# A fused attention and mixer kernel: the last 64 rows' sums in 128x32 strips behind the low-rank sums, and another order of the first slot

## The chip, the core and the metric

The kernel runs on one core of a Trainium2 chip. A core has five engines that run side by side, each through its own list of instructions: TensorE (PE) multiplies matrices into the accumulators (PSUM), VectorE (DVE), ScalarE (ACT) and GpSimd (POOL) work on elements, SyncE (SP) issues transfers. They wait for each other by semaphores. The metric is the device time of one execution in microseconds (us), the median of several executions. Three executions of the kernel before gave 979.51, 979.74 and 979.88 us: the median is 979.74 us.

## What is computed

```python
def _attn_ref(u, v, z):                     # u, v: 8 x 3136 x 256, z: 8 x 3136 x 64
    scores = (1.0 / S) * np.matmul(z, z.transpose(0, 2, 1))
    attn = np.maximum(scores, 0.0) ** 2
    return (u * np.matmul(attn, v)).astype(np.float32)

def _moe_ref(x, U, V, w_ch1, w_ch2):        # U: 3136 x 32, V: 32 x 3136
    h = x.transpose(0, 2, 1) @ U @ V
    u = x + h.transpose(0, 2, 1)
    ch = np.maximum(u @ w_ch1, 0.0) @ w_ch2 # 256 -> 1024 -> 256
    return (u + ch).astype(np.float32)
```

The output of the first is x of the second, for 8 batches b of 3136 rows. Matrices are multiplied in bf16 and summed in fp32.

## The kernel before

**Groups and slots.** The 3136 rows of a batch are 24 tiles of 128 rows and a tail of 64. Four tiles make a group, so a batch has six whole groups (g = 0 to 5) and the **small group** (g = NQ = 6) of the 64 tail rows. One (b, g) is an item, and the loop at L1395 runs one slot t for each of the 56 items. A slot holds the attention sums of its own item ("av", L668), the scores of a coming one (L428), the low-rank part of the item 7 slots back (`u2_unit`, L861) and the two channel products `ch1` and `ch2` of the item 8 slots back (L965, L1053).

**Order of the work.** The program is written out in the order in which it is recorded here; nothing reorders it. `emit` (L1159) walks through the slot's list of light units (one unit is a pair of matmuls of the av or the ch2 stream) and puts the units of the other queues in at the places that are given with them, if as many accumulators are free as the entry asks for. The kernel keeps a clock of its own (`clock`, `free_at`, `book`) by which it judges that, and by which `hold` puts off casts, squares and transfers. A matmul of 256 columns counts one unit of that clock.

**Accumulators.** There are four PSUM tiles of two banks (`take_ps`, L148). The av stream of a slot holds one throughout.

**Ways.** Most matmuls use 64 of the 128 rows of the array, two at a time: one on each half, each into another bank (`pair`, L179). To use both halves for both banks the stream goes through its data twice, in two ways (L640). At a change of ways a half must wait until the other half has done with the bank: an empty instruction on POOL (`post`, L170) waits for the last matmul, and the next matmul waits for it. What PE does between the two is one pair of scores or a transposition.

**Scores.** A pair of scores (two matmuls of 512 columns) must be scaled, cut off at zero and squared into bf16. `rectify` (L366) does so in one of three ways: "both" (ACT scales and cuts off, DVE squares), "dve" (DVE does both steps in two instructions, L397), "act" (ACT does both, L380, L381). In slot 0 it takes the ways that the list `ways` (L105) names, and when that is empty the one that the kernel's clock gives as the earliest. Batch 0 has nothing prepared, so in slot 0 the av stream uses blocks of scores just made, and z is turned on PE in four pieces (`z_turn`, L325); its last piece is the tail, whose casts `cast_tail` (L1314) makes on DVE. The six pieces of v of batch 0 are cast on POOL (L1307).

**The small group.** Its 64 rows are handled apart. `av_small` (L727) sums its attention in 52 matmuls on 64x64 quarters of the array, and `ch2_small` (L1139) its second channel product in 16; `four_sums` (L756) brings the four partial sums together (a copy on ACT, two additions on DVE). In the first slot of batches 2 to 7 both stand at place 72 of the av stream (L1474), `ch2_small` for the small group of two batches earlier. `t1_all` (L818) makes the low-rank sums U^T x of the batch before in 28 matmuls on four 128x32 strips of the array, at place 8 of the same slot (L1506); ACT copies half of the result, DVE adds the halves and doubles them (L847 to L849), and `u2_unit` at place 22 uses it. The batch's last piece of v is cast to bf16 in that slot too, by ACT (`cast`, L204).

Of the kernel before, what the change touches and what calls it, by code (L numbers as in the profile page):

```python
# [18 lines left out]
def kernel(  # L19
# [24 lines left out]
    GT = 4  # L44
# [60 lines left out]
    ways = ["both", "dve"]  # L105
# [260 lines left out]
    def rectify(dst, src, b, part=1, whole=False):  # L366
# [24 lines left out]
        return book("act", ready, 8.7 if part == 1 else 5.3), None  # L391
# [335 lines left out]
    def av_small(b, g):  # L727
        k, ps = take_ps()
        rows = groups[g][1]
        xs[b, g] = pool.tile([P, 1, D], BF16, name="x_small")  # L730
        nc.vector.memset(xs[b, g][rows:, 0, :], 0.0)
        for jt in range(NQ + 1):
            while (b, jt) not in v_cast:
                run_held(min(h[0] for h in held))
        for jt in range(NT + 1):
            c = jt % 2
            part = slice(0, D) if jt < NF else slice(c * D // 2, (c + 1) * D // 2)
            at = min(jt, NF)
            for h in range(2):
                nc.tensor.matmul(  # L740
                    out=ps[c * hp : c * hp + rows, h, part],
                    lhsT=smalls[b][h * hp : (h + 1) * hp, place_of(at), :],
                    rhs=v_bfs[b][h * hp : (h + 1) * hp, at, part],
                    start=(jt < 2),
                    stop=(jt >= NF),
                    tile_position=(h * hp, c * hp),
                )
        pe(NT / 2 + 2)
        u1 = u_sbs[b, g]
        four_sums(k, ps, u1[:rows, 1:3, :])  # L750
        nc.vector.tensor_tensor(
            out=xs[b, g][:rows, 0, :], in0=u1[:rows, 1, :], in1=u1[:rows, 0, :], op=ALU.mult
        )
        book("dve", clock[0] + 3, 3)

    def four_sums(k, ps, t):  # L756

        rows = t.shape[0]
        nc.scalar.copy(out=t, in_=ps[hp : hp + rows, :, :D])
        ready = book("act", clock[0] + 3, 5)  # L760
        nc.vector.tensor_tensor(out=t, in0=ps[:rows, :, :D], in1=t, op=ALU.add)  # L761
        ps_free[k] = book("dve", ready + 1, 6)
        nc.vector.tensor_tensor(out=t[:, 0, :], in0=t[:, 0, :], in1=t[:, 1, :], op=ALU.add)
        book("dve", ready, 4)
# [53 lines left out]
    def t1_all(b):  # L818
# [26 lines left out]
        up = pool.tile([P, D], FP32, name="t1_up", bufs=1)  # L845
# [15 lines left out]
    def u2_unit(b, g, turn=True):  # L861
# [145 lines left out]
    def small_relu(b, g):  # L1007

        return flat_of(relus[b, g][0])[:, : NH * groups[g][1]]

    def ch1_small(b, g, way, box):
# [4 lines left out]
        if way == 0:  # L1016
            relus[b, g] = [take_block()]
# [106 lines left out]
    def ch2_out(b, g, acc):  # L1124

        for e in relus.pop((b, g)):
            give_block(e)
# [10 lines left out]

    def ch2_small(b, g):  # L1139
        k, ps = take_ps()  # L1140
        rows = groups[g][1]
        for kt in range(NH):
            c = kt % 2
            for h in range(2):
                nc.tensor.matmul(  # L1145
                    out=ps[c * hp : c * hp + rows, h, :D],
                    lhsT=small_relu(b, g)[h * hp : (h + 1) * hp, kt * rows : (kt + 1) * rows],
# [435 lines left out]
```

## Time and profile before

| | |
|---|---|
| Median of three executions | 979.74 us |
| The profiled execution | 979.08 us |
| Its span, first to last instruction | 977.3 us |
| PE busy | 969.4 us (99%) |
| DVE busy | 633.7 us (65%) |
| ACT busy | 480.0 us (49%) |
| POOL busy | 15.7 us (2%) |
| First 20 us: PE, DVE, ACT, POOL busy | 17.22, 13.44, 15.63, 10.60 us |
| 20 to 40 us: the same | 19.15, 16.97, 17.31, 5.14 us |
| 400 to 600 us: PE busy | 200.00 us |
| 900 to 977 us: PE busy | 72.99 us |
| Granted TensorE clock in every one of these stretches | 1.00 |

The span is what the profiler saw between the first and the last instruction; the time of the execution lies 1.8 us above it. A median can be compared with another median, and a row of the profile with the span.

In a timeline each line gives the start of a row of equal instructions in us from the span's start, the time from the start of the first to the end of the last, the engine, the line of the kernel, the operation, what it writes and reads, the shape, and in brackets how long the engine had been idle before and what released it. A shape of 64\*128 is one on half the rows of the array, 64\*64 one on a quarter, 128\*32 one on a strip. The ends of matmuls overlap with the next ones; the distance between the starts of two rows is what counts.

### The profile page before, as it was taken

The page shows a single profiled execution, that of the slowest core. Times are in us where ns is not written, and L with a number is a line of the kernel's source. Part 1 is how long each engine was busy: PE and PEld are TensorE (multiplying, and loading weights), DVE is VectorE, ACT ScalarE, POOL GpSimd, SP SyncE. Part 2 cuts the span into 40 slices and gives each one's busy share as a digit, 9 for nine tenths or more (in the row PEclk, how much of TensorE's full clock was granted, in tenths as well). Part 3 has the DMA queues.
Part 4 walks back from the last instruction along what each step waited for, and adds up shares of the span by engine and source line. Part 5 has one row for each costly group of instructions (what it writes and reads, how often), then busy time and mean ns, then how long its engine had stood idle before and what let it go on. Part 6 is the DMA issues. An engine that isn't in the chain of part 4 may idle for free.

```text
span 977.3 us, 35450 instructions
## 1 busy us (share of the span) xinstructions
PE 969.4 (99%) x16211; PEld 774.7 (79%) x16211; DVE 633.7 (65%) x815; ACT 480.0 (49%) x562; POOL 15.7 (2%) x25
## 2 busy tenths in 40 slices
PE   8999999999999999999999999999999999999998
PEld 6798777887778777787778877788777888778765
DVE  6887865668556775557756577556765667653363
ACT  8877732457334563345543365433653346531353
POOL 4200000000000000000000000000000000000000
PEclk9999999999999999999999999999999999999999
DMA  9999899989988799997999679996999968974142
GB/s 271 193 202 223 207 208 209 201 192 182 198 211 161 182 197 189 210 147 186 182 222 195 139 185 198 213 185 131 198 213 202 192 133 183 179 137 101 50 116 98
DMA packets 372549, 176.37 MB, mean 180 GB/s; under 512 B 347312, under 2 KB 350896, under 8 KB 372400
## 3 DMA queue, kind: packets, MB, share of 16 engines
q1 hardware_dynamic: 372256, 173.98, 87.2%
q8 instruction: 126, 2.06, 0.9%
q14 instruction: 23, 0.19, 0.1%
q10 hardware_dynamic: 144, 0.13, 0.0%
HBM read 62.56 MB, written 25.69 MB: 90 GB/s over the span
## 4 chain that ended last, share of the span: by engine, by line
PE 98%; DVE 1%; ACT 0%; issue 0%; DVEq 0%
PE ps L184 95%; PE ps L740 1%; PE ps L825 1%; PE ps L1145 0%; ACT blk L390 0%; DVE blk L364 0%; PE ps L1349 0%; PE ps L331 0%; DVE blk L553 0%; DVE blk L397 0%; DVE x_bf L775 0%; ACT last_sb L390 0%; DVE blk L1113 0%; PE ps L542 0%; DVE blk L761 0%
## 5 line engine op out<-in xcount | busy, mean ns | idle before, releaser
L184 PEld LDWEIGHTS <-blk 64*128 64x128 bf16 x12288 | 610.9, 94 | 152.6 <-POOLq L174 8.9
L184 PE MATMUL ps<-v_bf,blk 64*128 64x256 bf16 x9216 | 610.2, 269 | 1.0 <-DVE blk L364 0.8
L390 ACT ACTIVATE blk<-ps 128x1024 bf16<-128x1024 f32 (+1 forms) x335 | 313.8, 969 | 344.0 <-PE ps L184 339.0
L364 DVE TENSOR_TENSOR blk<-blk 128x1024 bf16<-128x1024 bf16 x350 | 222.3, 658 | 46.2 <-ACT blk L390 45.6
L184 PE MATMUL ps<-u2T,w_bf 64*128 64x512 bf16 (+1 forms) x1792 | 226.2, 349 | 0.0
L1002 DVE TENSOR_SCALAR blk<-ps 128x1024 bf16<-128x1024 f32 x111 | 135.9, 1224 | 103.7 <-PE ps L184 102.8
L184 PE MATMUL ps<-w_bf,blk 64*128 64x256 bf16 x3072 | 189.8, 269 | 0.0
L1005 ACT ACTIVATE blk<-ps 128x1024 bf16<-128x1024 f32 x81 | 82.2, 1022 | 123.9 <-PE ps L184 120.1
L184 PE MATMUL ps<-zzT 64*128 64x512 bf16 (+2 forms) x898 | 128.1, 326 | 0.6 <-ACT zzT L340 0.6
L184 PEld LDWEIGHTS <-w_bf 64*128 64x128 bf16 x1792 | 82.2, 94 | 27.9 <-POOLq L174 5.2
L775 DVE TENSOR_TENSOR x_bf<-ps,u_sb 128x1024 bf16<-128x1024 f32 x48 | 58.7, 1222 | 68.4 <-PE ps L184 68.4
L910 DVE TENSOR_TENSOR out_sb<-ps,x_bf 128x1024 f32<-128x1024 f32 x42 | 51.4, 1223 | 57.4 <-PE ps L184 57.4
L1131 DVE TENSOR_TENSOR out_sb<-ps,out_sb 128x1024 f32<-128x1024 f32 x42 | 51.4, 1224 | 19.2 <-PE ps L184 19.2
L184 PEld LDWEIGHTS <-zzT 64*128 64x128 bf16 x898 | 41.6, 94 | 6.3 <-ACT zzT L340 0.8
L206 DVE CAST v_bf<-stage 128x1024 bf16<-128x1024 f32 (+1 forms) x35 | 21.5, 615 | 0.0
L386 DVE TENSOR_SCALAR blk<-ps 128x1024 bf16<-128x1024 f32 x14 | 17.1, 1223 | 6.5 <-PE ps L184 5.8
L184 PE MATMUL ps<-t_sb,V_bf 64*128 64x256 bf16 (+1 forms) x208 | 20.3, 265 | 0.0
L204 ACT CAST x_bf<-out_sb 128x1024 bf16<-128x1024 f32 x19 | 19.7, 1037 | 0.0
L184 PE MATMUL ps<-v_bf,last_sb 64*128 64x256 bf16 x192 | 18.5, 269 | 0.0
L1131 DVE TENSOR_TENSOR blk<-ps,blk 128x1024 f32<-128x1024 f32 x5 | 6.1, 1225 | 11.9 <-PE ps L184 11.8
L204 ACT CAST v_bf<-stage 128x1024 bf16<-128x1024 f32 x13 | 13.5, 1040 | 0.0
L626 ACT ACTIVATE attn_small<-ps 128x512 bf16<-128x512 f32 (+1 forms) x32 | 13.1, 499 | 0.0
(86 smaller groups left out, 239.1 us busy)
## 6 DMA issues: line engine op xcount, KB each, us to landing
u_sb<-in_u_dram SPq DMA_DIRECT2D x48, 512.0 KB, 5.1
stage<-in_v_dram SPq DMA_DIRECT2D x42, 512.0 KB, 6.4
out_dram<-out_sb SPq DMA_DIRECT2D x42, 512.0 KB, 3.1
stage<-in_z_dram SPq DMA_DIRECT2D x7, 512.0 KB, 6.3
blk<-in_v_dram SPq DMA_DIRECT2D x5, 512.0 KB, 6.1
out_dram<-blk SPq DMA_DIRECT2D x5, 512.0 KB, 2.8
blk<-blk SPq DMA_TRANSPOSE x156, 5.1
blk<-in_moe_w_ch_dram SPq DMA_DIRECT2D x4, 512.0 KB, 5.5
```

The costliest lines, as they stand in the source:

```text
L184: ins = nc.tensor.matmul(**args)
L204: nc.scalar.copy(out=out, in_=in_)
L206: nc.vector.tensor_copy(out=out, in_=in_)
L364: nc.vector.tensor_tensor(out=a, in0=a, in1=a, op=ALU.mult)
L386: nc.vector.tensor_scalar(out=dst, in0=src, scalar1=scale, scalar2=0.0, op0=ALU.mult, op1=ALU.max)
L390: nc.scalar.activation(out=dst, in_=src, func=AF.Relu, scale=scale)
L626: nc.scalar.activation(out=dst[:, jj], in_=src[:, jj], func=AF.Relu, scale=scale)
L775: nc.vector.tensor_tensor(out=xs[b, g][:rows, :n, :], in0=four(box["ps"])[:rows, :n, :], in1=u_sbs[b, g][:rows, :n, :], op=ALU.mult,)
L910: nc.vector.tensor_tensor(out=o, in0=four(ps), in1=x, op=ALU.add)
L1002: nc.vector.tensor_single_scalar(out=r, in_=ps[:, :, :gw], scalar=0.0, op=ALU.max)
L1005: nc.scalar.activation(out=r, in_=ps[:, :, :gw], func=AF.Relu)
L1131: nc.vector.tensor_tensor(out=o, in0=acc, in1=o, op=ALU.add)
```

## The change

1. `av_small`, `four_sums` and `ch2_small` are replaced by `small_sums`. It makes the sums of the small group on four 128x32 strips (`in_strips`), 32 of the 64 rows to a strip and every second tile to the other pair of strips, as many matmuls of the same columns as before: 16 for the second channel product into bank 0 (argument `second`, a batch), 52 for the attention into bank 1 (argument `first`). One copy, one addition and the final instructions follow.
2. In the first slot of batches 2 to 7 `both_sums` calls `t1_all` and right behind it `small_sums`, at place 8. The channel product is now that of three batches earlier, so the small group's `relu_small` and `out_small` get buffers of their own, which live a batch longer. `u2_unit` moves from place 22 to 12, and the load of `u_small` from 130 units into the slot before to 10. Batches 0 and 1 keep their attention sums where they were, in strips; the last three channel products stand behind `t1_all` of the last batch and in the last part.
3. In the first slot (t = 0) two pairs of scores stand at four of the five changes of ways that had one, and single pairs at five places in the stream where there were nine. `ways` names ten choices instead of two. The kernel's clock counts 9.3 for ACT's step in slots 0 and 1 where it counted 8.7. `cast_tail` casts on POOL.

```diff
     slot = [0]
-    ways = ["both", "dve"]
+    ways = ["both", "dve", "both", "both", "both", "dve", "both", "both", "both", "dve"]
...
         else:
-            t = pool.tile([P, 3, D], FP32, name="u_small", bufs=1)
+            t = pool.tile([P, 1, D], FP32, name="u_small", bufs=1)
...
             dve += 6.5 * waiting[0]
-            ends = {"dve": dve + DVE, "act": act + 19, "both": max(act + 8.7, dve) + 7.5}
+            ends = {"dve": dve + DVE, "act": act + 19, "both": max(act + 9.3, dve) + 7.5}
...
         nc.scalar.activation(out=dst, in_=src, func=AF.Relu, scale=scale)
-        return book("act", ready, 8.7 if part == 1 else 5.3), None
+        return book("act", ready, 5.3 if part != 1 else 9.3 if slot[0] < 2 else 8.7), None
...
-    def av_small(b, g):
+    def in_strips(ps, bank, lhs, rhs, n, odd):
+
+        m = P // NREP
+        for i in range(n):
+            whole = i < n - 1 or not odd
+            for c in range(NREP) if not whole else (i % 2 * 2, i % 2 * 2 + 1):
+                w = c % 2
+                part = slice(0, D) if whole else slice(c // 2 * D // 2, (c // 2 + 1) * D // 2)
+                nc.tensor.matmul(
+                    out=ps[c * m : (c + 1) * m, bank, part],
+                    lhsT=lhs(i, slice(w * m, (w + 1) * m)),
+                    rhs=rhs(i)[:, part],
+                    start=(i < 2),
+                    stop=(i >= n - 2 if not odd else not whole),
+                    tile_position=(0, c * m),
+                )
+        pe(n / 2 + 1)
+
+    def small_sums(second, first, into=None):
+
         k, ps = take_ps()
...
-    def four_sums(k, ps, t):
...
+        rows = groups[NQ][1]
+        if second is not None:
+            in_strips(
+                ps,
+                0,
+                lambda i, w: small_relu(second, NQ)[:, i * rows : (i + 1) * rows][:, w],
+                lambda i: w2_bf[:, i, :],
+                NH,
+                False,
+            )
+        if first is not None:
+            b = first
+            xs[b, NQ] = pool.tile([P, 1, D], BF16, name="x_small")
+            nc.vector.memset(xs[b, NQ][rows:, 0, :], 0.0)
+            for jt in range(NQ + 1):
+                while (b, jt) not in v_cast:
+                    run_held(min(h[0] for h in held))
+            in_strips(
+                ps,
+                1,
+                lambda i, w: smalls[b][:, place_of(i), w],
+                lambda i: v_bfs[b][:, i, :],
+                NT,
+                True,
+            )
+        at, end = 0 if second is not None else 1, 2 if first is not None else 1
+        n = end - at
+        t = (into or sums_tile())[:rows]
+        nc.scalar.copy(out=t[:, at:end], in_=ps[hp : hp + rows, at:end, :D])
+        ready = book("act", clock[0] + 3, 1 + 2 * n)
+        nc.vector.tensor_tensor(out=t[:, at:end], in0=ps[:rows, at:end, :D], in1=t[:, at:end], op=ALU.add)
+        ps_free[k] = book("dve", ready + 1, 1 + 2.5 * n)
+        if first is not None:
+            nc.vector.tensor_tensor(
+                out=xs[first, NQ][:rows, 0, :], in0=t[:, 1, :], in1=u_sbs[first, NQ][:rows, 0, :], op=ALU.mult
+            )
+            book("dve", clock[0] + 3, 3)
+        if second is not None:
+            ch2_out(second, NQ, t[:, 0:1, :])
+            book("dve", clock[0] + 3, 3)
...
-    def t1_all(b):
+    def sums_tile():
+        return pool.tile([P, GT, D], FP32, name="out_sb", bufs=3)
+
+    def both_sums(b, second, first):
+        t = sums_tile()
+        t1_all(b, t)
+        small_sums(second, first, t)
+
+    def t1_all(b, into=None):
...
-        up = pool.tile([P, D], FP32, name="t1_up", bufs=1)
+        up = (into or sums_tile())[:, 2, :]
...
             o = raw.rearrange("p (q d) -> p q d", d=D)
+        elif n < GT:
+            o = pool.tile([P, 1, D], FP32, name="out_small", bufs=2)
...
-        return flat_of(relus[b, g][0])[:, : NH * groups[g][1]]
+        return relus[b, g]
...
         if way == 0:
-            relus[b, g] = [take_block()]
+            relus[b, g] = pool.tile([P, NH * gw], BF16, name="relu_small", bufs=1)
...
-        for e in relus.pop((b, g)):
-            give_block(e)
+        e = relus.pop((b, g))
+        if g < NQ:
+            for x in e:
+                give_block(x)
...
-    def ch2_small(b, g):
...
         for c in range(2):
-            on_dve(out=z_bfs[0][:, NF, c, :], in_=raw[:, 2 * GT * dqk : n * dqk])
-        v_tail(0, n, raw, on_dve)
-        book("dve", clock[0], 5)
+            on_pool(out=z_bfs[0][:, NF, c, :], in_=raw[:, 2 * GT * dqk : n * dqk])
+        v_tail(0, n, raw, on_pool)
...
         if t > NG and g_now == NQ and b_next < B:
-            hold(clock[0] + 60 + 70, lambda b=b_next: load_u(b, NQ))
+            hold(clock[0] + 10, lambda b=b_next: load_u(b, NQ))
...
             if t == NG:
-                qc.append((64, 2, False, lambda: av_small(1, NQ)))
-            if fin:
-                qc.append((72, 2, False, lambda: (ch2_small(*fin), av_small(att[0], NQ))))
+                qc.append((64, 2, False, lambda: small_sums(None, 1)))
             k = min(2, len(mine) // 3)
             n = len(mine) - 3 * k
             at = [1 + 80 * i / n for i in range(n)]
             if t == 0:
-                at, k = [16, 30, 46, 50, 64, 68, 78, 84, 92], 0
+                at, k = [16, 50, 64, 78, 84], 0
                 qs += [(4, 0, True, lambda: scores(1)), (12, 0, True, lambda: z_turn(0, 2 * GT, on_act))]
-                qs += [(x, 0, True, lambda: scores(1)) for x in (24, 40, 56, 72, 88)]
+                qs += [(x, 0, True, lambda x=x: scores(1 if x == 56 else 2)) for x in (24, 40, 56, 72, 88)]
...
-            small = (lambda: None) if early(*att) else (lambda: av_small(*att))
+            small = (lambda: None) if early(*att) else (lambda: small_sums(None, att[0]))
...
                 else:
-                    order = up + [small, c0, c1, d0, d1, c2, c3, lambda: t1_all(att[0]), d2, d3]
+                    order = up + [small, c0, c1, d0, d1, c2, c3, lambda: both_sums(att[0], B - 3, None), d2, d3]
             qc += [(0, 0, False, f) for f in order]
         if av and u2i:
             if u2i[1] == 0:
-                qm.append((8, 1, False, lambda: t1_all(u2i[0])))
-            qm.append((22 if u2i[1] == 0 else 40, 1, False, lambda: u2_unit(*u2i)))
+                sums = t > NG
+                b = att[0]
+                qm.append(
+                    (
+                        8,
+                        2 if sums else 1,
+                        False,
+                        lambda: both_sums(b - 1, b - 3 if b > 2 else None, b) if sums else t1_all(b - 1),
+                    )
+                )
+            qm.append((40 if u2i[1] else 12 if sums else 22, 1, False, lambda: u2_unit(*u2i)))
...
             if k == 1 or k == NQ:
-                qm.append((9, 1, False, lambda b=B - 2 if k == 1 else B - 1: ch2_small(b, NQ)))
+                qm.append((9 if k == 1 else 5, 1, False, lambda b=B - 2 if k == 1 else B - 1: small_sums(b, None)))
```

More of the change, by code (lines that the diff above doesn't have):

```diff
@@ L723, in av_stream @@
         return Ways(2 * NF, 1, step, box)
-    def av_small(b, g):
-        k, ps = take_ps()
[L729 to L754, printed above, removed]
@@ L756, in four_sums @@
-    def four_sums(k, ps, t):
[L758 to L764, printed above, removed]
+    def in_strips(ps, bank, lhs, rhs, n, odd):
[14 more added lines that the diff above has]
+        pe(n / 2 + 1)
@@ L1136, in ch2_out @@
             give_block(o_blocks.pop((b, g)))
-    def ch2_small(b, g):
[L1140 to L1147, printed above, removed]
-                    rhs=w2_bf[h * hp : (h + 1) * hp, kt, :],
-                    start=(kt < 2),
-                    stop=(kt >= NH - 2),
-                    tile_position=(h * hp, c * hp),
-                )
-        pe(NH / 2 + 2)
-        sums = u2s[b, g][:rows, 1:3, :]
-        four_sums(k, ps, sums)
-        ch2_out(b, g, sums[:, 0:1, :])
-        book("dve", clock[0] + 3, 3)
     def emit(light, queues, av=None, slack=14, hurry=14):
```

## The prediction

> **What bounds the kernel now.** I read the page's busy times first, then the chain that ended last, then PE's timeline where the change works.
>
> ```profile
> span 977.3 us, 35450 instructions
> PE 969.4 (99%) x16211; PEld 774.7 (79%) x16211; DVE 633.7 (65%) x815; ACT 480.0 (49%) x562; POOL 15.7 (2%) x25
> ...
> PE 98%; DVE 1%; ACT 0%; issue 0%; DVEq 0%
> ```
>
> PE is the bound and hardly pauses: 7.9 us of the span are idle, of them 3.6 in the first 40 us and 4.0 in the last 77 (mostly the last output on its way). After 40 us PE's busy time equals the time, so a gain there can only come from matmuls that take less time, not from shorter waits. Both programs have 16211 matmuls of the same columns. What can differ is how densely they stand. The timeline of a batch's first slot (b = 2):
>
> ```profile
> 212.36 0.93 PE L184 MATMUL ps<-v_bf,blk 64*128 64x256 bf16 x14
> 213.22 0.84 PE L825 MATMUL ps<-x_bf,U_bf 128*32 128x256 bf16 x24
> 213.89 0.20 PE L835 MATMUL ps<-x_small,U_bf 128*32 128x64 bf16 x4
> 214.02 1.05 PE L184 MATMUL ps<-v_bf,blk 64*128 64x256 bf16 x16
> ...
> 221.91 1.36 PE L184 MATMUL ps<-v_bf,blk 64*128 64x256 bf16 x22
> 223.20 0.63 PE L1145 MATMUL ps<-w_bf,blk 64*64 64x256 bf16 x16
> 223.66 1.54 PE L740 MATMUL ps<-v_bf,attn_small 64*64 64x256 bf16 x52
> 225.13 1.05 PE L184 MATMUL ps<-v_bf,blk 64*128 64x256 bf16 x16
> ```
>
> Compare starts. In the long streams a pair of 256 columns takes 0.1094 us (22 of them: 11 pairs, 1.20). From 221.91 that gives 223.11, but the 64x64 matmuls begin at 223.20: 0.09 lost on entering another division of the array. They are 68 matmuls in fours, 17 x 0.1094 less half a step for the four of 128 columns = 1.81; they took 1.93 up to 225.13. With 0.01 in the first pair behind, a stretch of 64x64 costs 0.23 us beyond its columns. The strips cost the same: 0.09 before 213.22, 0.80 for 0.68 of columns (six fours and 64 columns), 0.01 behind: 0.23. Within a stretch strips and quarters run alike, four matmuls in 0.1094 to 0.112.
>
> In the first slot PE does wait. The chain of waits there:
>
> ```profile
> 16.90 1.55 PE ps L184 x22
> 18.46 0.01 issue
> 18.47 0.23 PE ps L331
> ...
> 20.48 1.02 ACT last_sb L390
> 21.50 2.76 ACT blk L390 x3
> ...
> 24.89 1.22 DVE x_bf L775
> 26.11 0.61 DVE blk L364
> ...
> 26.77 4.63 PE ps L184 x70
> ```
>
> Between 20 and 26 us the chain runs over ACT's scaling and DVE, not over PE: scores are made barely in time. From the starts of PE's rows, the waits for DVE's squares are 0.20 at 16.90, 0.21 at 19.72, 1.01 at 26.77, 0.17 at 31.40 and 0.16 at 32.01 us: 1.75 in all. Five changes of ways with one pair of scores between cost 0.066 us each.
>
> **The change, part by part.**
>
> *Fewer divisions.* Counted in the built programs, stretches of 64x64 or 128x32 fall from 18 to 12: in the first slots of batches 2 to 7 two become one. 6 x 0.23 = **-1.38 us**. The new strips have the form of L825 (128 rows, 32 columns, 256 moving), so I take that row's pace; the weights change as often.
>
> *A cast that is needed sooner.* The attention sums move from place 72 to behind `t1_all`, and need all of v. The last piece is cast by ACT, and the built program puts that cast right behind ACT's copy of the low-rank sums:
>
> ```profile
> 214.15 0.37 ACT L847 COPY t_up<-ps 64x256 f32<-64x256 f32 x1 [0.55 <-PE ps L835]
> ...
> 214.42 1.04 ACT L204 CAST v_bf<-stage 128x1024 bf16<-128x1024 f32 x1
> ```
>
> So v is whole at 215.46, 1.57 after L835's start (213.89). Strips begin 0.03 after that start. In batches 3 to 7 the 16 matmuls of `ch2` go first (0.44), then 40 of attention (1.09) before the 41st needs the piece: 1.56, against 1.57 and some 0.05 for the semaphore: 0.05 lost. In batch 2 there is no `ch2` part: 1.12 against 1.62, 0.50 lost. Sum **+0.75**. Behind PE nothing else of ACT waits then. The bounds are 0, if the clock of the kernel lets the cast go a little earlier, and +1.8, if one of ACT's scalings (1.02, L390) slips in front of it once.
>
> *The results of the sums.* One copy (0.58, L759's form), one addition (0.68) and two short ones (0.42 each) on DVE follow, and in front of `u2_unit`'s addition (1.22). PE's next scores want the accumulator back 1.53 us after the strips end; copy and addition take 0.12 + 0.58 + 0.03 + 0.68 = 1.41. No wait, by 0.1 us; DVE has some 35% of idle time to take the rest. If the cover goes, it is 0.15 a batch. Buffers, the earlier `u_small` load and the stores are SP's; the load lands 5 us after its issue in the profile and has a slot more time, so I put them at nothing, and so the end of the program, where the order of the last pieces on PE, DVE and SP stays.
>
> *The first slot,* by the built program's order and the durations of rows: ACT's scaling 1.02 (the next starts 0.93 later), DVE's two steps 1.22 and 0.69, ACT's square 1.05 (no row; L554's 128x512 square took 0.63 where the same-sized scaling took 0.59, so a little over 1.02; the bounds are 0.9 and 1.2). I number PE's matmuls.
> - Until 145 the two pairs at the change save 0.07. Matmul 147 is the first of a second pair, and needs z's next piece, which ACT had copied at 15.12: it starts at 15.16 where it was free at 14.82. At 165 PE is 0.21 behind; the old wait of 0.20 at 16.90 falls away (DVE's square ends at 16.93), so 183 starts at 17.43, before 17.35.
> - Matmul 197 turns z's tail. Its casts now stand on POOL behind two casts of v:
>
> ```profile
> 17.69 1.23 POOL L1310 CAST v_bf<-blk 128x512 bf16<-128x512 f32 x2 [1.50 <-PE ps L184]
> 17.70 0.71 DVE L1317 CAST z_bf<-blk 128x64 bf16<-128x64 f32 x2
> ```
>
>  POOL's casts of v wait for the same change of ways, so they run 17.77 to 19.00, and z's two follow, at 0.1 each (an eighth of 0.61, and a little): 19.2. PE starts 197 at 19.27, not 18.47: **0.8 behind**.
> - The scores behind it come later too. ACT gets its next pair at 21.18 (20.48 before) and has in order three scalings with their squares, now on ACT, and one more scaling: 7 steps, to 28.26; DVE's square of that pair ends at 28.97, and matmul 318 needs it: 29.03, before 27.43. The waits at 242 (0.4) and 294 (0.4) lie inside that.
> - The old waits at 31.40 and 32.01 shrink to 0.2: matmul 394 at 34.04, before 32.56. One more doubled change saves 0.07. From there nothing waits: **+1.4**.
>
> Bounds: all 1.75 of waits and 4 x 0.066 gone, -2.0; or POOL and DVE slow each other, below, +3.0.
>
> Sum: -1.38 + 0.75 + 1.4 = +0.77 on the profiled execution's 979.08 (977.3 of span and 1.78 around it), 979.85. The median lies 0.66 above that execution, so 980.5.
>
> **The rivals.** I call a difference under 0.2% (1.96 us) no change; a measurement of this kernel tells about that.
> 1. *Faster: the first slot becomes dense.* If the tail's cast is ready at about 18.5 (POOL gets to it before v) and the sharing keeps ACT ahead, the waits of 1.75 and the 0.26 go: 979.74 - 1.38 + 0.75 - 2.0 = 977.1. For it: ACT worked without a pause from 21.40 to 26.33, and three scalings leave it there. Against it: three squares come instead, and the order on POOL is fixed.
> 2. *Slower: POOL and DVE get in each other's way.* In the profile a 128x64 cast on DVE took 0.19 and the next one 0.61 beside POOL's cast, and a square at 28.36 took 1.25 instead of 0.69. If one waits out the other, a square ahead of POOL's second cast of v puts z's tail at 19.9 (+0.7), the squares before 394 are late by 0.5 beside POOL's casts at 29.6 to 32, and those behind by 0.4 beside its casts near 35: 1.4 + 1.6 = 3.0, and 979.74 + 3.0 - 0.63 = 982.1. It decides from +2.6 in the first slot on. Against it: there POOL's two took 0.68 and 0.61. The Trainium skill (SBUF — State Buffer, section "SBUF: two separate sides") says that the port pair which VectorE and GpSimd share is "an **exclusive lock**, not a bandwidth split", held for the whole instruction. By that rule this rival is the rule and not the accident; the 0.61 and the 1.25 agree with it, POOL's undisturbed 0.61 at 18.31 doesn't decide.
> 3. *It does not save the division.* A merged stretch might drain between banks or between `t1_all` and the sums: without the -1.38 the sum is 981.9. Against it: L1145 and L740 follow each other in the profile in another accumulator with no loss.
>
> **How the numbers follow.** Forecast (within 0.2%): 0.43. Rival 1 and other gains: 0.25. Rival 2 0.27, rival 3 0.05, together slower 0.32. The time is 980.5; its own range is 978.6 (first slot at -0.5) to 981.7 (at +2.6, where rival 2 begins). The range over the cases goes from 976.9, just under rival 1, to 982.6, which is rival 2 with the cover of 0.15 lost in three of the six merged stretches.
>
> **What would show it.** Right: six stretches of 80 or 96 strips with one loss of 0.1 at each end; a wait of 0.5 for the cast in batch 2 and hardly any in the others; in the first slot PE waiting for POOL near 19.2 and for a DVE square near 29; no PE wait after 35 us. Wrong: z's tail turned before 18.8; a PE start of 318 before 28; strips slower than 0.115 per four; or waits of PE inside the steady slots, which the profile before has none of.

## The result, and the profile after

The changed kernel took **983.06 us** (median of seven executions, 982.63 to 984.60), the kernel before 979.88 (979.51 to 981.09) beside it on the same chip. The ratio is **1.0033, 95% interval 1.0024 to 1.0043**: slower by about 3.2 us. The prediction had 980.5 and a range of 976.9 to 982.6. The profiled execution of the changed kernel took 983.06.

Its page: span, busy times, and the chain of waits by engine.

```profile
span 981.3 us, 35422 instructions
PE 969.2 (99%) x16211; PEld 798.4 (81%) x16211; DVE 622.6 (63%) x792; ACT 476.4 (49%) x556; POOL 16.1 (2%) x28
...
PE 94%; DVE 1%; ACT 1%; DMA 1%; SPq 0%; issue 0%; DVEq 0%; ACTq 0%
```

PE is busy for 969.2 us where it was 969.4, DVE and ACT are busy for less, POOL for 0.4 more, and the span is 4.0 us longer. So the added time is not added work: PE stands idle for longer, and the chain now goes over DMA too, which it did not before. The view of what PE waited for in the whole span gives the places, first in the kernel before, then in the changed one (zzT holds the turned z, t_sb the low-rank sums, u2T the turned rows that `ch1` multiplies; SPq in other listings is SP issuing a transfer):

```profile
PE ps L184 <- DVE blk L364: 0.8, 1, 0.8
...
PE ps L184 <- ACT zzT L340: 0.6, 1, 0.6
PE ps L331 <- POOL z_bf L242: 0.2, 1, 0.2
```

```profile
PE ps L184 <- DMA u2T<-x_small: 1.7, 1, 1.7
PE ps L331 <- POOL z_bf L1332: 1.4, 1, 1.4
PE ps L184 <- DVE blk L364: 1.3, 2, 1.0
...
PE ps L184 <- ACT zzT L340: 0.4, 1, 0.4
PE ps L735 <- ACT v_bf L204: 0.3, 1, 0.3
PE ps L184 <- ACT blk L380: 0.3, 1, 0.3
PE ps L184 <- DVE t_sb L879: 0.2, 1, 0.2
PE ps L184 <- DVE blk L1035: 0.2, 1, 0.2
```

The columns are: us in total, how often, and the longest. Four of these lie in the first slot (POOL z_bf, DVE blk L364, ACT blk L380, and zzT at 10.4 us, which was 0.6 before). Of the others only v_bf was foreseen: the rest are a transposition that is late near 930 us, t_sb at 99.6 and L1035 at 127.9. What a wait costs is more than the idle time shown, because the profile models the ends of matmuls and idle time counts from them: from start to start, the idle 1.36 at L331 cost 1.52, 0.33 at v_bf cost 0.51, 0.17 at t_sb cost 0.33, 1.73 at u2T cost 1.90, that is 0.165 to 0.176 more each time.

Both programs have the same number of matmuls with the same columns, so the starts of equal places can be subtracted. Distances between starts on PE, in us (the first three by PE's matmul numbers, the others from the first matmul of a batch's low-rank sums to that of the next):

| Stretch | before | after | difference |
|---|---|---|---|
| matmul 145 to 199 (z's tail is turned) | 3.96 | 5.61 | +1.65 |
| 199 to 321 (the scores behind it) | 8.91 | 9.67 | +0.76 |
| 97 to 1400 in all (slots 0 to 6) | 78.78 | 81.04 | +2.26 |
| 1400 to batch 1's low-rank sums | 122.90 | 123.88 | +0.98 |
| batch 1's to batch 2's | 119.50 | 119.65 | +0.15 |
| each next to the one of batch 6 | 119.50 | 119.35 to 119.40 | -0.10 to -0.15 |
| batch 6's to batch 7's | 111.13 | 110.65 | -0.48 |
| batch 7's to the last matmul | 50.89 | 53.21 | +2.32 |

Two rows move work over their edges: `ch2` of a small group (16 matmuls, 0.44) leaves the row of 119.65 and arrives in the last one, and the low-rank sums stand six matmuls later in the order (0.31), which is in the row of 123.88 and comes off at 110.65. Without these: +0.67 in batch 1, +0.59 in the next row, +1.88 at the end.

### The profile page after: what moved, and what is told of

It is laid out like the page before. It is cut to its first block, busy times and chain, and to the rows that moved or that the text cites. A ratio compares the mean times of both kernels' runs of the same rounds, so it can differ in the third digit from the quotient of the medians.

```text
span 981.3 us, 35422 instructions
## 1 busy us (share of the span) xinstructions
PE 969.2 (99%) x16211; PEld 798.4 (81%) x16211; DVE 622.6 (63%) x792; ACT 476.4 (49%) x556; POOL 16.1 (2%) x28
## 4 chain that ended last, share of the span: by engine, by line
PE 94%; DVE 1%; ACT 1%; DMA 1%; SPq 0%; issue 0%; DVEq 0%; ACTq 0%
PE ps L184 92%; PE ps L735 1%; PE ps L856 1%; DVE blk L364 0%; DMA stage<-in_v_dram 0%; DVE blk L1035 0%; DMA u2T<-x_small 0%; ACT blk L390 0%; SPq L220 0%; ACT blk L1038 0%; SPq L412 0%; DVE w_bf L206 0%; ACT v_bf L204 0%; ACT w_bf L204 0%; ACT out_sb L878 0%
## 5 line engine op out<-in xcount | busy, mean ns | idle before, releaser
L184 PEld LDWEIGHTS <-blk 64*128 64x128 bf16 x12288 | 632.6, 94 | 133.4 <-POOLq L174 8.2
L390 ACT ACTIVATE blk<-ps 128x1024 bf16<-128x1024 f32 (+1 forms) x330 | 310.1, 967 | 349.3 <-PE ps L184 331.7
L364 DVE TENSOR_TENSOR blk<-blk 128x1024 bf16<-128x1024 bf16 x348 | 218.4, 653 | 49.2 <-ACT blk L390 48.6
L1035 DVE TENSOR_SCALAR blk<-ps 128x1024 bf16<-128x1024 f32 x111 | 135.9, 1224 | 112.8 <-PE ps L184 112.8
L184 PEld LDWEIGHTS <-w_bf 64*128 64x128 bf16 x1792 | 85.4, 94 | 27.6 <-POOLq L174 5.1
L184 PEld LDWEIGHTS <-zzT 64*128 64x128 bf16 x898 | 44.0, 94 | 6.4 <-ACT zzT L340 1.2
L735 PE MATMUL ps<-v_bf,attn_small 128*32 128x256 bf16 (+1 forms) x416 | 12.9, 269 | 0.3 <-ACT v_bf L204 0.3
```

The costliest lines, as they stand in the source:

```text
L184: ins = nc.tensor.matmul(**args)
L364: nc.vector.tensor_tensor(out=a, in0=a, in1=a, op=ALU.mult)
L390: nc.scalar.activation(out=dst, in_=src, func=AF.Relu, scale=scale)
L735: nc.tensor.matmul(out=ps[c * m : (c + 1) * m, bank, part], lhsT=lhs(i, slice(w * m, (w + 1) * m)), rhs=rhs(i)[:, part], start=(i < 2), st ...
L1035: nc.vector.tensor_single_scalar(out=r, in_=ps[:, :, :gw], scalar=0.0, op=ALU.max)
```

## The experiments

Each ratio is to the kernel before on the same chip, with its 95% interval. Executions on these chips scatter more than in the first runs (the kernel before from 979.3 to 982.5), among other things because matmul 97 starts anywhere from 11.3 to 13.0 us into the span (one profiled execution of each kernel). Distances from matmul 97 on are free of that, and carry the readings below.

### The first slot, and one store at the end

The first kernel takes all edits of the first slot back (item 3 of the change). The second takes nothing back but the place of one store on SP's queue:

```diff
-        nc.sync.dma_start(out=dst, in_=o)
-        queued(n * rows)
+        def store():
+            if (b, g) == (B - 3, NQ) and (B - 2, NQ) not in u2Ts:
+                hold(clock[0] + 1, store)
+                return
+            nc.sync.dma_start(out=dst, in_=o)
+            queued(n * rows)
+
+        store()
```

The third does both, the fourth puts the edits of the first slot alone into the kernel before.

> The changed kernel with the first slot as it was (two given ways, single pairs at the changes, z's tail cast by VectorE, 8.7 in the booking). Theory: the first slot alone lost 2.12 us and nothing else depends on it, so the time is 983.06 - 2.1 = 980.95, and PE still waits 0.33 at the zzT matmuls behind the low-rank sums of batch 0 (99.61 in the changed kernel), 0.32 at the ch1 matmuls near 127.87, and 1.7 for the transposition of x_small near 930. Rival: the two waits of batch 1 come from a clock of the kernel that the first slot shifted; then they go too, 980.3. Second rival: the loss of the first slot is made up again later, and the time stays at 982.5 or above.

> The changed kernel with one DMA moved on SP's queue: the store of batch 5's small group is issued behind the transposition of batch 6's x_small in place of ahead of it; PE's program is the same matmul for matmul. Theory: the transposition waited on SP behind that store, which waits for VectorE's addition ending at 927.0; issued at about 924.3 it lands at 927.6, under the first use, and the 1.90 us that PE lost at 930.05 go: 981.15, the PE wait for u2T<-x_small gone. Rival: the transposition itself is slow there because the DMA engines are busy with stores; then it still lands after 928.3 and PE still waits 0.5 or more: 981.7 to 983.0.

> Both edits: the first slot as it was and the store behind the transposition; what is left of the change is the sums in 128x32 strips and their place. Theory: the two losses lie in different stretches and add up: 983.06 - 2.12 - 1.90 = 979.0, 0.8 under the kernel before, as the five merged stretches of batches 3 to 7 save 0.12 to 0.16 each and the two waits of batch 1 and batch 2's wait for the cast stay. Rival: the strips cost as much as they save, 979.6 to 980.1. Second rival (the waits of batch 1 leave with the first slot): 978.4.

> The kernel before with the first slot's edits alone (the given ways, two pairs at the changes, z's tail cast by GpSimd, 9.3 in the booking); the sums stay in 64x64 quarters in their old places. Theory: the first slot loses 2.12, 982.0, with z's tail turned at 19.9 and PE waiting 1.2 for a square near 29.6. Rival: later waits follow from it too (0.64 in batch 1): 982.6. Second rival: the first slot only loses in company with the other edits: 979.9 to 980.5.

| Kernel | median, us | ratio | matmul 97 to 1400 | batch 7's low-rank sums to the end |
|---|---|---|---|---|
| first slot as before | 981.45 | 1.0012 (1.0003 to 1.0021) | 78.91 | 53.21 |
| store behind the turn | 982.16 | 1.0019 (1.0011 to 1.0028) | 81.09 | 51.59 |
| both | 979.45 | 0.9993 (0.9984 to 1.0003) | 79.05 | 51.53 |
| first slot alone | 982.95 | 1.0027 (1.0016 to 1.0039) | 81.09 | 51.40 |

The two losses are independent and add up, as expected: from matmul 97 to 1400 the first slot costs 2.0 to 2.3 whatever the sums do, and at the end the store costs 1.6 to 1.7. In ratios the theories had 1.0011, 1.0013, 0.9991 and 1.0022. The first and the third came out so; the medians of the second and the fourth lie at or next to their rivals' values (1.0019 to 1.0032, and 1.0028), though the rivals' reasons fit only in part: in the second a small wait is left at the transposition, and in the fourth PE loses 0.18, 0.29 and 0.50 near 129, 348 and 930 us. The timeline at the end of the kernel before, where that transposition leaves as soon as x_small is cast:

```profile
921.60 0.39 ACT L204 CAST x_small<-out_sb 64x256 bf16<-64x256 f32 x1
922.02 1.18 SPq L811 DMA_TRANSPOSE u2T<-x_small  x1
...
925.49 0.40 PE L184 MATMUL ps<-u2T,w_bf 64*128 64x64 bf16 x16
```

In the changed kernel:

```profile
923.84 0.39 ACT L204 CAST x_small<-out_small 64x256 bf16<-64x256 f32 x1
...
926.58 0.42 DVE L1166 TENSOR_TENSOR out_small<-out_sb,out_small 64x256 f32<-64x256 f32 x1
927.02 0.53 SPq L1168 DMA_DIRECT2D out_dram<-out_small  x1
927.66 1.18 SPq L834 DMA_TRANSPOSE u2T<-x_small  x1
...
930.05 0.41 PE L184 MATMUL ps<-u2T,w_bf 64*128 64x64 bf16 x16 [1.73 <-DMA u2T<-x_small]
```

and the same with the store behind the transposition (matmul 97 starts 1.6 us later in it, so compare distances):

```profile
925.47 0.39 ACT L204 CAST x_small<-out_small 64x256 bf16<-64x256 f32 x1
925.89 1.17 SPq L834 DMA_TRANSPOSE u2T<-x_small  x1
...
928.66 0.52 SPq L1172 DMA_DIRECT2D out_dram<-out_small  x1
930.07 0.41 PE L184 MATMUL ps<-u2T,w_bf 64*128 64x64 bf16 x16
```

x_small was ready to be transposed at 924.23. SP takes its queue in order, and in front stood the store of batch 5's small group, which `both_sums` had brought there and which waits for DVE's addition up to 927.00. So the transposition left 3.4 us after its data were ready, and in the second listing at once. PE's program is the same in both. 0.28 of loss is left there, since 4.1 pass from its issue to its landing, where 3.4 passed in the kernel before, which had no wait there. That rest is not the store's: in the ten kernels with strips and the moved store the landing took 3.65 to 4.30 and PE lost 0 to 0.44, and in the fourth kernel, whose sums stand in their old places, it took 3.92 and PE lost 0.50. In the kernel before, it landed 0.06 ahead of PE's start, so the place had no margin to begin with.

The wait for t_sb in batch 1 did not leave with the first slot (0.33 at L879 stands in all three kernels with strips and not in the fourth): it belongs to the sums. The other, at L1035, can't be placed so: its idle time is 0.04, 0.34 and none in the three, and PE loses 0.18 there in the fourth.

### The parts of the first slot

The kernel with both taken back is the base here; to it come, one each: all edits of the slot but the tail's casts; those casts on GpSimd alone; the list `ways` alone; the two pairs at a change alone.

```diff
-            on_dve(out=z_bfs[0][:, NF, c, :], in_=raw[:, 2 * GT * dqk : n * dqk])
-        v_tail(0, n, raw, on_dve)
-        book("dve", clock[0], 5)
+            on_pool(out=z_bfs[0][:, NF, c, :], in_=raw[:, 2 * GT * dqk : n * dqk])
+        v_tail(0, n, raw, on_pool)
```

> Strips and moved store kept, and of the first slot all edits but one: z's tail is cast by VectorE as before. In the run with the first slot as before the time stood 0.7 us under the kernel before; the whole first slot cost 2.12. Theory: GpSimd's late casts (z's tail ready at 19.86, PE losing 1.52 at its turn) are most of the first slot's loss, since the stalls behind it only hand it on: without them 0.6 to 1.0 of the 2.12 is left, and the time is 0.1 under to 0.3 over the kernel before; PE loses under 0.3 at the turn of z's tail. Rival: ACT's chain of three scalings and three squares sets the end of the slot whatever the tail does; then 1.7 to 2.1 is left, 1.0 to 1.4 over the kernel before, with a wait of PE for a square of some 2 us near 29.

> Strips and moved store kept, the first slot as before but for z's tail, which GpSimd casts behind its two casts of v. Theory: POOL's casts of v take 0.85 each beside a square on VectorE, the tail is turned at 19.7 to 19.9, PE loses 1.2 to 1.5 there, and ACT's later scalings, which the kernel before had no pause in, hand on nearly all of it: 0.4 to 0.8 over the kernel before (against 0.7 under it with the whole old slot). Rival: the stall at the tail is taken back at the wait of 1.01 near 26.77, whose length is set by ACT's chain from an earlier point: then 0.2 to 0.7 under the kernel before.

> Strips and moved store kept, the first slot as before but for the list of given ways (ten in place of two; single pairs at the changes, tail on VectorE). Theory: sharing by the list costs little by itself: PE's waits for squares sum to 1.5 to 2.1 as in the old slot (1.75), and the time is 0.9 to 0.3 under the kernel before. Rival: the list is what loses time, since it hands VectorE the scalings of 1.22 when a square is due and ACT three squares of 1.06: 0.5 to 1.4 over the kernel before, with the wait near 27 to 29 at 2 us or more.

> Strips and moved store kept, the first slot as before but for the places of its scores: two pairs at four of the five changes of ways in place of one, and five single places in place of nine. Theory: four changes fewer save 4 x 0.066 = 0.26, but second pairs wait for z's next piece and for ACT (0.3 at matmul 147); about even: 1.0 to 0.4 under the kernel before. Rival: two pairs at once put ACT behind, and PE's waits for squares grow by 0.5 or more: 0 to 0.8 over the kernel before.

| Kernel | median, us | ratio | 145 to 199 | 199 to 321 | 321 to 1400 | 97 to 1400 |
|---|---|---|---|---|---|---|
| before | | | 3.96 | 8.91 | 62.78 | 78.78 |
| both taken back | 979.45 | 0.9993 (0.9984 to 1.0003) | 4.46 | 8.69 | 62.78 | 79.05 |
| all but the tail's casts | 981.75 | 1.0014 (1.0005 to 1.0023) | 4.08 | 9.44 | 64.03 | 80.61 |
| tail's casts on GpSimd | 981.35 | 1.0007 (0.9999 to 1.0016) | 5.68 | 8.69 | 62.78 | 80.28 |
| given ways | 980.08 | 0.9993 (0.9984 to 1.0002) | 4.43 | 9.55 | 62.78 | 79.90 |
| two pairs | 979.67 | 0.9992 (0.9983 to 1.0000) | 3.94 | 9.02 | 62.78 | 79.13 |

(In the second row z's tail was late, 0.51 of idle time, and half of that was made good behind. Its two casts on VectorE took 1.20 beside GpSimd's casts of v, where the same ones took 0.71 in the kernel before and in the run with the first slot as before.) So the costs that follow are counted from the first row. The tail on GpSimd costs 1.7 in its own stretch and 1.5 in all. Two pairs cost 0.1 or nothing (the rest of 79.13 lies ahead of matmul 145). The list costs 1.1 in this profile, of which one wait for a square at 17.18 makes half; the medians do not resolve it. The medians of the last three rows lie where their theories had them. For the first kernel the time came out as the rival had it, but not for its reason: no wait of 2 us stands near 29, and 1.25 of its 1.83 lies behind matmul 321, in stalls at 34.4, 38.8 and 44.2 us that no other kernel has. Taking the casts back also takes back their entry in the kernel's clock, and that shifts the order of what follows: 88 matmuls up to number 695 are others than in the run with the moved store. So this run could not say what the tail costs, and a further one was made: the changed kernel (with the store moved), and the tail's casts ahead of GpSimd's casts of v.

```diff
-                qm.append((58, 0, False, cast_tail))
+                qm.append((54, 0, False, cast_tail))
```

> The changed kernel with the store behind the transposition, and z's tail cast by GpSimd ahead of its two casts of v in place of behind them (its place on the list of the first slot 54 for 58). The same kernel without this edit stood at a ratio of 1.0019, and its stretch from matmul 97 to matmul 1400 took 81.09 us against 78.78 before. Theory: the order on GpSimd made the tail late, but ACT's chain of scalings and squares is the other limit and lies only a little behind: with the tail on VectorE 80.61 were left; so the stretch takes 80.5 to 80.9, PE loses under 0.8 at the turn of z's tail, the waits for squares grow, and the ratio is 1.0013 to 1.0018. Rival: with the tail early the whole stall of 1.45 is saved, 79.6 to 79.8, and the ratio is 1.0004 to 1.0007.

It took 980.97, **ratio 1.0001 (0.9992 to 1.0010)** against 1.0019 without the edit: the rival was right, and the theory of a second limit close behind was wrong. GpSimd and PE's turn in the changed kernel, then with the tail first:

```profile
17.77 0.69 DVE L364 TENSOR_TENSOR blk<-blk 128x1024 bf16<-128x1024 bf16 x1 [0.22 <-ACT blk L390]
17.79 1.71 POOL L1325 CAST v_bf<-blk 128x512 bf16<-128x512 f32 x2 [1.38 <-PE ps L184]
...
19.45 0.41 POOL L1332 CAST z_bf<-blk 128x64 bf16<-128x64 f32 x2
...
19.91 0.23 PE L331 MATMUL ps<-ident,z_bf 128*128 128x128 bf16 x1 [1.36 <-POOL z_bf L1332]
```

```profile
17.29 0.42 POOL L1338 CAST z_bf<-blk 128x64 bf16<-128x64 f32 x2
...
19.09 1.63 POOL L1331 CAST v_bf<-blk 128x512 bf16<-128x512 f32 x2 [0.58 <-PE ps L184]
...
19.79 0.23 PE L331 MATMUL ps<-ident,z_bf 128*128 128x128 bf16 x1
```

In the first, POOL stood idle for 1.38 us until PE let it go on, then cast v beside DVE's square, then z. In the second the tail was done at 17.71, and PE turned it with no wait. The stretch from 145 to 199 fell from 5.42 (the same kernel without the edit) to 4.12, that from 199 to 321 stayed at 9.67: the order on GpSimd cost 1.3. Independent of it, 0.76 is left for the other edits of the slot, most of it the given ways by their own row. (The edit also moves three matmuls between 242 and 278.)

### The cast of v, and two waits in batch 1

Three steps on the base with both taken back. First ACT's cast of v's last piece is made due sooner; then the accumulator of batch 0's low-rank sums is booked for longer; then one transposition goes back behind two loads on SP.

```diff
-            hold(clock[0] + (90 if g_now == NQ and b_next > 1 else 45 if t == NG + 1 else 15 if t >= NQ else 45) + 12 * i, f)
+            hold(clock[0] + (78 if g_now == NQ and b_next > 1 else 45 if t == NG + 1 else 15 if t >= NQ else 45) + 12 * i, f)
...
-        ps_free[k] = book("dve", clock[0] + 10, 6)
+        ps_free[k] = book("dve", clock[0] + (10 if into else 16), 6)
...
-            if free_at["sp"] > now + (30 if needed(e)[0] <= slot[0] + 1 else 0):
+            if free_at["sp"] > now + (30 if needed(e)[0] <= slot[0] + 1 else -4 if slot[0] == NG else 0):
```

> First slot as before and store behind the transposition, and the casts of a batch's last pieces of v due 12 units of the kernel's clock sooner (78 for 90), which puts ACT's cast in front of its copy of the low-rank sums. Theory: the strips of batch 2 wait 0.51 and those of batches 3 to 7 0.07 each for that cast alone; both go, 0.86 in all, and the time is 1.5 us under the kernel before (0.9985), against 0.7 without this edit. Rival: the cast of 1.04 in front delays the copy of the low-rank sums, and PE then waits for t_sb or for the accumulator behind the strips by as much: 0.2 to 0.9 under the kernel before.

> As the run with the cast sooner, and the accumulator of batch 0's low-rank sums booked 6 units longer in the kernel's clock, so that the second zzT pair behind them comes 14 matmuls after the first as in the kernel before, not 2 after it. Theory: the wait of 0.33 for t_sb L879 near 98 came from that place alone and goes: 1.8 us under the kernel before (0.9981), and no PE wait between 95 and 101. Rival: the wait moves to the next matmuls that want an accumulator, and nothing is gained over the run with the cast sooner.

> As the run with cast and booking, with one transposition of blk on SP put back behind the loads of u_sb and of a piece of v in batch 1's first slot, where the kernel before has it; PE's program is the same matmul for matmul. Theory: that transposition blocks SP for 7.8 us, so the two loads of 512 KB start at 114.8 and share the DMA engines with the tails of z and v, ACT's cast of z's piece waits 1.9 for its DMA, and the scalings behind it make PE wait 0.79 at 124.86 and 0.52 at 126.69; with the loads first these waits go and the stretch from the 1400th matmul to batch 1's low-rank sums is 123.2 to 123.4 us against 124.52: 2.2 to 2.8 us under the kernel before, ratio 0.9972 to 0.9978. Rival: the waits near 125 come from the places of the scores on PE, or from DMA that varies from run to run; then 0.5 or more of them stays and the ratio is 0.998 or above.

| Kernel | median, us | ratio | 1400 to batch 1's sums | batch 1's to 2's | the next four |
|---|---|---|---|---|---|
| before | | | 122.90 | 119.50 | 119.50 |
| both taken back | 979.45 | 0.9993 (0.9984 to 1.0003) | 123.63 | 119.35 | 119.35 |
| cast sooner | 979.02 | 0.9983 (0.9974 to 0.9992) | 124.32 | 118.83 | 119.27 |
| and booking | 979.22 | 0.9984 (0.9975 to 0.9993) | 124.52 | 118.83 | 119.27 |
| and loads first | **977.62** | **0.9968 (0.9956 to 0.9981)** | 123.21 | 118.83 | 119.27 |

(The last column leaves out one value each of the second and the fourth row, 119.54 and 119.55, by one loss near 345 us that has no releaser in the profile.) The cast gave what was expected: 0.52 in batch 2 and 0.08 in each of the next, and PE waits nowhere in the strips. The strips of batch 2 in the changed kernel, then with the cast in front:

```profile
217.01 1.26 PE L735 MATMUL ps<-v_bf,attn_small 128*32 128x256 bf16 x40
217.24 0.37 ACT L878 COPY out_sb<-ps 64x256 f32<-64x256 f32 x1 [0.88 <-PE ps L866]
217.51 1.04 ACT L204 CAST v_bf<-stage 128x1024 bf16<-128x1024 f32 x1
218.60 0.46 PE L735 MATMUL ps<-v_bf,attn_small 128*32 128x256 bf16 x12 [0.33 <-ACT v_bf L204]
```

```profile
215.71 1.04 ACT L204 CAST v_bf<-stage 128x1024 bf16<-128x1024 f32 x1
...
216.46 1.54 PE L735 MATMUL ps<-v_bf,attn_small 128*32 128x256 bf16 x52
216.77 0.37 ACT L878 COPY out_sb<-ps 64x256 f32<-64x256 f32 x1
217.93 0.28 PE L184 MATMUL ps<-v_bf,blk 64*128 64x256 bf16 x2
```

The copy of the low-rank sums now starts 0.31 behind the start of these strips where it started 0.23 behind it, and PE waits for neither. A batch lasts 119.27 where it lasted 119.50: **0.23, the price of one stretch of another division**, is saved in full.

The booking took the wait for t_sb away, as expected, but near 125 PE lost more (1.31 in place of 0.77), so nothing was gained in all; the rival had the outcome, though not the place. The third step shows what stands behind the loss near 125. In the kernel before the two loads go first:

```profile
110.48 0.33 SPq L308 DMA_DIRECT2D u_sb<-in_u_dram  x1
...
110.91 0.94 SPq L256 DMA_DIRECT2D stage<-in_v_dram  x1
...
111.90 4.59 SPq L420 DMA_TRANSPOSE blk<-blk  x1
```

SP's queue, ACT's cast of z and PE near 125 us, without the third step:

```profile
106.97 7.76 SPq L420 DMA_TRANSPOSE blk<-blk  x1
...
114.83 0.52 SPq L308 DMA_DIRECT2D u_sb<-in_u_dram  x1
115.44 0.39 SPq L256 DMA_DIRECT2D stage<-in_v_dram  x1
...
117.63 1.72 SPq L220 DMA_DIRECT2D stage<-in_z_dram  x2
...
123.22 0.67 ACT L204 CAST z_bf<-stage 128x576 bf16<-128x576 f32 x1 [1.92 <-DMA stage<-in_z_dram]
...
124.86 1.49 PE L184 MATMUL ps<-w_bf,blk 64*128 64x256 bf16 x24 [0.62 <-ACT blk L390]
```

and with the loads first:

```profile
111.70 0.33 SPq L308 DMA_DIRECT2D u_sb<-in_u_dram  x1
...
112.13 0.81 SPq L256 DMA_DIRECT2D stage<-in_v_dram  x1
112.99 4.70 SPq L420 DMA_TRANSPOSE blk<-blk  x1
...
122.78 0.67 ACT L204 CAST z_bf<-stage 128x576 bf16<-128x576 f32 x1 [0.48 <-DMA stage<-in_z_dram]
...
125.08 1.91 PE L184 MATMUL ps<-w_bf,blk 64*128 64x256 bf16 x32
```

Behind the transposition the two loads of 512 KB leave at 114.8 and 115.4, just ahead of the tails of z at 117.6, and these take 5.2 and 4.4 from issue to landing; ACT's cast waits 1.92 for them, its scalings behind the cast are late, and PE waits. With the loads at 111.7 and 112.1 the tails of z take 3.2 and 2.1, the cast waits 0.48 and PE's 32 matmuls run through. PE's program is the same matmul for matmul. The order isn't all of it. In the eleven kernels that have the transposition in front, ACT's wait at this cast goes from 0.68 to 1.92, and PE loses in this stretch, besides the wait for t_sb, about as much as that wait exceeds 0.6: 0.09 at 0.68, 0.34 at 0.93 in the changed kernel, 1.31 at 1.92. In the three kernels with the loads in front it is 0.32, 0.48 and 0.80, and only the last of them loses anything. So the order accounts for most of the loss, and how the transfers come in an execution sets its size; that the booking made it larger is not shown. Why the transposition came in front is argued, not shown: the new sums count less in the kernel's clock, so that SP counts as free a few units earlier, and an edit of 4 units puts it back.

This kernel (five executions) is faster than both the changed one and the kernel before: 1.9 to 4.3 us under the latter by its interval. From matmul 97 to the last it takes 960.01 against 961.21, 1.20 less, and from there to the end 0.56 less; the rest of the difference of the medians (2.7) is not shown by these two profiles.

## Why the prediction was wrong, step by step

**Fewer divisions, -1.38: right.** 0.23 a batch, once the cast is out of the way. Merged stretches do not drain between accumulators, so the third rival fell. The Trainium skill (TensorEngine Tiling (Array Packing), section "Key Properties") says that a change of the tiling mode drains TensorE, without a price; that each stretch saved gave 0.23 agrees.

**A cast that is needed sooner, +0.75: right.** 0.52 and 5 times 0.08 are 0.92, at the places named.

**"Results of the sums": right as far as it went.** PE waits for none of the copies and additions behind the merged sums. The wait for t_sb (0.33) is in batch 1, where nothing is merged: there a pair of scores moved from 12 matmuls behind another pair to 2, because a booked time changed; with the longer booking it stands 14 behind, and the wait is gone.

**The first slot, +1.4: the mechanism was right, one term too small.** Matmul 1400 came 2.1 late. Matmul 197 was to turn z's tail 0.8 late, and was 1.4 late. The step that failed is "they run 17.77 to 19.00, and z's two follow, at 0.1 each": beside DVE's square the two casts of v took 1.71, not 1.23, and z's two 0.41. Putting the tail first took 1.3 of the slot's loss away. The next step, 0.8 for the scores up to matmul 318, came out at 0.76. The second rival had z's tail at 19.9, which is the time measured; its other terms, 1.6 of late squares further on, did not come.

**"Buffers, the earlier `u_small` load and the stores are SP's ... I put them at nothing, and so the end of the program, where the order of the last pieces on PE, DVE and SP stays": wrong, and the largest error.** The order on SP did not stay. A store that waits for DVE came in front of a transposition that PE waits for, 1.90; and in batch 1 a transposition came in front of two loads, 0.32 here and 0.1 to 1.3 in other runs. Both stand in the order of SP's queue, which the prediction read nowhere but in the profile of before. The upper end of the range, 982.6, held none of this, and the time lies 0.5 above it.

In sum: +0.77 was predicted. To this come 0.7 for the first slot, nearly all of it GpSimd's casts, 1.9 for the store, 0.65 for the two waits of batch 1, 0.17 more for the cast and 0.30 for one wait at 225.76 that has no releaser in the profile: 4.5, and PE's last matmul is 4.6 later. The span grew by 4.0 only, as the way from there to the end became 0.6 shorter, 3.7 in place of 4.3. Its sign "no PE wait after 35 us" failed by the waits near 99.6, 127.9 and 930. The medians differ by 3.2 and not by 4.0 because the profiled execution of the kernel before lies 0.8 under its median and that of the changed kernel at its median.

## What to carry to other kernels

Where sums, stores or anything that issues a transfer is moved, read the queue of the issuing engine at the new place, in the built order: whatever stands behind a store that waits for a late result waits too. Where a planner decides by a clock of its own, a changed booking is a change of the order elsewhere; the two waits of batch 1 took back 0.65 of the 1.38 that the merged stretches saved. A cast given to an idle engine is only as early as that engine's queue: here it stood behind two casts and a wait for PE, and moving it by four places on a list was worth 1.3 us.

## What was not expected of the hardware

A wait on PE costs 0.165 to 0.176 us more than the idle time that the profile shows (seven places of the changed kernel, from 0.03 to 1.73 of idle time). Nearly all of that follows from how the rows are made: the profile gives a matmul of 256 columns 0.269 us, and one of 512 columns 0.376, so 256 columns count 0.107 and 0.162 comes on top in each, while in a dense stream a pair of matmuls of 256 columns starts every 0.109. Read what a wait costs from starts. The Trainium skill (TensorE: Matmul & The Clock Gate, section "Single matmul latency") gives a constant of 166 ns for a single warm matmul on top of its columns. The rows agree with it, but since their ends are modelled they are no independent test of it.

GpSimd and VectorE lengthened each other. Two casts of 128x512 on POOL took 1.17 to 1.24 without, 1.63 to 1.71 with a square beside them, and a square that took 0.69 alone took 1.07 in the run with the store moved. The Trainium skill (SBUF — State Buffer, section "Who interferes with whom") says that an operation of VectorE with two inputs in SBUF and one of GpSimd that reads SBUF block each other for whole instructions. Two casts and a square one after the other would be 1.86 to 1.92; in that run the two casts were through in 1.63 and the square beside them in its 1.07, so by these rows, which are rough on POOL and overlap at their ends, it is nearly but not quite that. The same work can come out either way: VectorE's two casts of z's tail, beside GpSimd's two casts of v, took 0.71 in the kernel before and 1.20 in the run with both taken back; what decides that is not shown.

A transposition by DMA held SP's queue for 4.7 us behind two loads and for 7.8 in front of them, so its place on the queue decides over more than its own data. What it waits for in that time, no run here shows.
